# One more transpose per head quad, layer norm sums on VectorE, and another order list, in an interleaved four-layer kernel

## The chip, the cores and the metric

The kernel runs on one core of one Trainium2 chip. The metric is device time in microseconds (us): 3121.67 us is the median of 3 runs before the change (3118.93 to 3122.74). One of these executions, the one of 3118.93 us, was profiled, and all durations below are from that profile.

## The reference

Four layers with residuals act on one sequence of 2048 tokens of 640 numbers, in the order A, B, A, B, with the same weights for both A layers and for both B layers.

```
x = x + _A_ref(_layernorm(x), A_mem0, A_Wq, A_Wk, A_Wv, A_Wo, A_seg_len)
x = x + _B_ref(_layernorm(x), B_wqkv, B_wo)
x = x + _A_ref(_layernorm(x), A_mem0, A_Wq, A_Wk, A_Wv, A_Wo, A_seg_len)
x = x + _B_ref(_layernorm(x), B_wqkv, B_wo)
```

Layer A goes through 64 segments of 32 tokens, one after the other. Each segment has 8 memory rows before it, so 40 rows; q, k and v have 32 heads of 192 numbers; after softmax, weighting and the output projection, the first 8 rows become the memory of the next segment. This chain from segment to segment cannot be cut. Layer B is attention over 8 earlier tokens at distance 0, 2, ..., 14, with 32 heads of 20 numbers.

## The kernel before the change, in words

**Steps.** A loop of 67 steps runs everything (`run`, L841, and `step`, L809). In step t the first A layer works on segment t and, beside it, the second A layer on segment t-2: two lanes of 40 rows, 80 rows in all (`NT`). The B layers of the step before run in the gaps. Steps 0, 1, 64 and 65 have one lane (40 rows); steps 2 to 63 have both; the last step has B alone. Everything is kept transposed: the 640 or 768 features lie on partitions in chunks of 128, the rows run along the free dimension.

**One step of layer A** goes through 8 quads of heads (768 columns of each weight). The pieces, by their names in the list, are: `K`, `Q`, `V` (30 matmuls each, 128x128 weights against 80 rows, L315), their copies out of PSUM `KE` (ScalarE, L341), `QE` (VectorE, L347 and L349) and `VE` (ScalarE, L355 and L357); `T`, transposes of v on TensorE (L369); `TE` and `TF`, which copy the transposed v into its tile `Vt` (VectorE L377 and L379, ScalarE L387); `S`, the scores (6 matmuls, L397); `E`, exp on ScalarE (L403); `EM`, the mask on VectorE (L409); `PO`, probabilities times v (8 matmuls, L430), whose columns of ones in `Vt` give the sums; `R`, one over the sums by Ln and Exp on ScalarE (L417, L419); `OT1` and `OT2`, the scaled outputs on VectorE (L437; L442, L443); `Oa` and `Ob`, the output projection, 15 matmuls each (L449), of which quad 6's second half is cut into `O6x` and `O6y`, and quad 7's into `O7x`, `O7y`, `O7z`. `Oa` of a quad needs rows that `OT1` writes, `Ob` those of `OT2` too. At the end of a step `LSQ`, `lst`, `LMV`, `LR`, `LAP` make the layer norm of the next segment, `MEMa` and `MEMb` (L488) copy the new memory rows into the next step's input, and `X1` adds the residual for layer B. `K0` of the next step can start only when `LAP` and `MEMa` are done. Lower-case pieces are layer B's, from its layer norm (`bsq`, `bst`, `bmv`, `br`, `bap`) over its projections (`bq`, `bk`, `bv`) and attention to `by`.

**Transposes of v before the change.** v of a quad is 6 chunks of 80 rows, 480 columns. Here they are packed into 5 tiles of 128 columns: one chunk (80 columns) is cut into three strips of up to 32, which fill the last 32 columns of three other tiles (the second copy of `vE`). So 5 transposes do. `tF` then moves the three strips to their partitions with three ScalarE copies.

**Layer norm sums before the change.** `ln_sq` (L490) forms the sum of x over the 5 chunks on GpSimd with three additions (L496), and the square and the sum of squares on VectorE (L500, L501); then it splits both sums into high and low halves (L503, L504) for a matmul against ones. In the last step `b_rows` restricts the work to the one lane that is left.

**What sets the order.** Nothing is scheduled by a tool: each engine executes its instructions in the order of the list `ORDER` (L49), one list for all steps with layer A, and `LAST` (L60) for the final step. PSUM tiles rotate through four banks (`big`), and the P·V result and the reciprocal tile have one buffer each.

**Weights.** Layer A's weights are 128 pieces of 256 or 224 KB. 78 stay in SBUF after step 0; the other 50 are read again in every step through a ring of 8 buffers, by DMAs that SyncE issues in the order of use. `resident_pieces` (L97) chooses the 50 so that they lie evenly in the list. So a new list also moves these DMAs.

Of the kernel before, what the change touches and what calls it, by code (L numbers as in the profile page):

```python
# [17 lines left out]
P = 128  # L18
D = 640
# [23 lines left out]
V_AT = (1, 0, 2, 3, 5, 4)  # L43

# [5 lines left out]
K0 bsq K0y KE0 Q0 V0 QE0 bst Q1 S0 bmv VE0 QE1 E0 T0 br K1 TE0 KE1 TF0 V1 Q2 VE1 EM0 S1 PO0 bap QE2 E1 V2 R0  # L50
EM1 T1 K2 VE2 TE1 OT10 bq TF1 OT20 K3 KE2 KE3 bqE PO1 bk R1 K4 S2 KE4 E2 T2 bkE Q3 TE2 bs0 Q4 TF2 bv be0 bvE
OT11 QE3 bs1 be1 EM2 QE4 V3 OT21 eb0 S3 PO2 VE3 E3 eb1 EM3 R2 bt K5 KE5 T3 btE V4 Q5 TE3 TF3 VE4 Oa1 S4 OT12
bp1 OT22 QE5 E4 PO3 on1 EM4 R3 V5 T4 VE5 TE4 K6 OT13 Q6 S5 TF4 OT23 bp0 PO4 KE6 Oa0 Ob0 E5 QE6 on0 T5 R4 S6
TE5 EM5 OT14 E6 V6 TF5 OT24 Q7 QE7 VE6 bo Ob1 PO5 boE T6 by TE6 R5 K7 TF6 byE EM6 KE7 OT15 V7 OT25 VE7 S7 PO6
Oa2 E7 LSQ T7 Ob2 R6 Oa3 EM7 lst TE7 OT16 Ob3 Oa4 TF7 OT26 LMV PO7 Oa6 Oa5 O6x R7 OT17 OT27 Ob4 Ob5 O6y LR LAP
O7x O7y MEMa O7z MEMb X1
# [4 lines left out]
bsq bst bmv br bap bk bkE bq bqE bv bs1 be1 bvE eb1 bt btE bp0 on0 bp1 on1 bo boE by byE  # L61
# [62 lines left out]
class Kernel:  # L124
    def __init__(self, ctx, tc, xT, m0T, wA, wqkv, wo, out):

        self.tc = tc
        self.nc = tc.nc
        self.x = xT
        self.mem0 = m0T  # L130
        self.wA = wA
        self.b_src = (wqkv, wo)
        self.out = out
        self.n_seg = 2 * xT.shape[0]
        pool = lambda name, bufs, **kw: ctx.enter_context(tc.tile_pool(name=name, bufs=bufs, **kw))
        self.cp = pool("consts", 1)
        self.wres = pool("wres", 1)
        self.wring = pool("wring", RING)
        self.ap1 = pool("act1", 1)
        self.ap2 = pool("act2", 2)  # L140
        self.bp = pool("bact", 1)
        self.xp = pool("xio", 1)
        self.ps_one = pool("ps_one", 1, space=PSUM)
        self.units = {}
        self.place = {u: n for n, u in enumerate(half_order())}
        self.resident = resident_pieces()
        self.cur = {}
        self.n_big = 0
        self.bl = range(2)
        self.xt, self.ots, self.qxs, self.kp, self.qp, self.vp, self.tp = {}, {}, {}, {}, {}, {}, {}  # L150
        self.x_load(0)
        self.build_consts()

    def build_consts(self):
# [33 lines left out]
        self.VT = pers("VT", [P, NC, P], 1)[0]  # L188
# [112 lines left out]
    def span_of(self, t):  # L301

        self.l0 = 0 if t < self.n_seg else 1
        self.l1 = 2 if t >= LAG else 1
        self.cs = slice(LT * self.l0, LT * self.l1)
        self.bl = range(2)

    def proj(self, ps, kind, i, h, t, chained=False):

        hT = self.hT[t % 2]  # L310
        c0, c1 = self.cs.start, self.cs.stop
        for k, (c, n) in enumerate(half_blocks(kind, i, h)):
            yield k
            n = V_AT[n] if kind == "v" else n
            self.nc.tensor.matmul(ps[:, NT * n + c0:NT * n + c1], lhsT=self.block(kind, i, h, k), rhs=hT[:, NT * c + c0:NT * c + c1],  # L315
                                  start=(h == 0 and k == 0) if chained else c == 0, stop=(c == NC - 1), skip_group_check=chained)
# [35 lines left out]
    def vE(self, i):  # L352

        ps, cs, copy = self.vp[i], self.cs, self.nc.scalar.copy
        copy(out=self.VT[:, :, cs], in_=ps[:, NT:6 * NT].rearrange("p (a n) -> p a n", a=NC)[:, :, cs])  # L355
        if cs.stop - cs.start == NT:
            copy(out=self.VT[:, 0:3, P - 32:P], in_=ps[:, 0:96].rearrange("p (a n) -> p a n", a=3))  # L357
        else:
            for j in range(3):
                a, b = max(cs.start, 32 * j), min(cs.stop, 32 * (j + 1))  # L360
                if a < b:
                    copy(out=self.VT[:, j, P - 32 + a - 32 * j:P - 32 + b - 32 * j], in_=ps[:, a:b])

    def a_t(self, i):

        nc = self.nc
        ps = self.big("ps_vt", (P, NC, P), BF16)
        for n in range(NC):
            nc.tensor.transpose(out=ps[:, n, :], in_=self.VT[:, n, :], identity=self.ident[:])  # L369
        self.tp[i] = ps  # L370

    def tE(self, i):

        nc = self.nc
        ps = self.tp[i]
        dst = self.Vt[0:NT].rearrange("p (a j e) -> p a j e", a=2, e=P)
        nc.vector.tensor_copy(out=dst[:, :, 0:4:3, :], in_=ps[0:NT, 0:4, :].rearrange("p (a j) e -> p a j e", a=2))  # L377
        two = lambda v: v.rearrange("p (j e) -> p j e", j=2)[:, :, 0:64]
        nc.vector.tensor_copy(out=two(self.Vt[0:NT, 640:896]), in_=ps[0:NT, 4, :].rearrange("p (j e) -> p j e", j=2))  # L379

    def tF(self, i):

        ps = self.tp[i]
        two = lambda v: v.rearrange("p (j e) -> p j e", j=2)[:, :, 0:64]
        for j in range(3):
            n = min(NT - 32 * j, 32)
            self.nc.scalar.copy(out=two(self.Vt[32 * j:32 * j + n, 128:384]), in_=ps[96:96 + n, j, :].rearrange("p (j e) -> p j e", j=2))  # L387
# [102 lines left out]
    def ln_sq(self, x):  # L490

        nc = self.nc
        sq = self.bp.tile([P, NC, NX], BF16, name="sq", tag="sq")
        ns = self.b_rows()
        s = self.bp.tile([P, 4, NX], F32, name="ln_s", tag="xc")
        add = lambda out, a, b: nc.gpsimd.tensor_tensor(out=out, in0=a, in1=b, op=ALU.add)  # L496
        add(s[:, 2:4, ns], x[:, 0:2, ns], x[:, 2:4, ns])
        add(s[:, 2, ns], s[:, 2, ns], s[:, 3, ns])
        add(s[:, 0, ns], s[:, 2, ns], x[:, 4, ns])
        nc.vector.tensor_tensor(out=sq[:, :, ns], in0=x[:, :, ns], in1=x[:, :, ns], op=ALU.mult)  # L500
        nc.vector.tensor_reduce(out=s[:, 1, ns], in_=sq[:, :, ns].rearrange("p c n -> p n c"), op=ALU.add, axis=mybir.AxisListType.X)  # L501
        hl = sq[:].rearrange("p c n -> p (c n)")[:, 0:4 * NX].rearrange("p (j a n) -> p j a n", j=2, a=2)
        nc.vector.tensor_copy(out=hl[:, 0, :, ns], in_=s[:, 0:2, ns])  # L503
        nc.vector.tensor_tensor(out=hl[:, 1, :, ns], in0=s[:, 0:2, ns], in1=hl[:, 0, :, ns], op=ALU.subtract)  # L504
        return hl

    def ln_stats(self, hl):
        nc = self.nc
        ps = self.big("ps_st")
        for j in range(2):  # L510
            nc.tensor.matmul(ps[:, 0:2 * NX].rearrange("p (a n) -> p a n", a=2)[:, :, self.b_rows()], lhsT=self.ones[:], rhs=hl[:, j, :, self.b_rows()],
                             start=(j == 0), stop=(j == 1))
        return ps

    def ln_mv(self, ps):

        nc = self.nc
        ns = self.b_rows()
        m = self.bp.tile([P, NX], F32, name="ln_m")
        nc.vector.tensor_scalar(out=m[:, ns], in0=ps[:, ns], scalar1=1.0 / D, scalar2=None, op0=ALU.mult)  # L520
        v = self.bp.tile([P, NX], F32, name="ln_v")
        nc.vector.tensor_tensor(out=v[:, ns], in0=m[:, ns], in1=m[:, ns], op=ALU.mult)
        nc.vector.scalar_tensor_tensor(out=v[:, ns], in0=ps[:, NX + ns.start:NX + ns.stop], scalar=1.0 / D, in1=v[:, ns], op0=ALU.mult, op1=ALU.subtract)
        return m, v

    def ln_r(self, mv):
# [3 lines left out]
        ns = self.b_rows()  # L530
        nc.scalar.activation(out=v[:, ns], in_=v[:, ns], func=ACT.Ln, bias=self.eps_t[:])
        r = self.bp.tile([P, NX], F32, name="ln_r")
        nc.scalar.activation(out=r[:, ns], in_=v[:, ns], func=ACT.Exp, scale=-0.5)
        return m, r

    def ln_big(self, x, mr, dst):
# [4 lines left out]
        ns = self.b_rows()  # L541
        nc.vector.tensor_tensor(out=xc[:, :, ns], in0=x[:, :, ns], in1=m[:, ns].unsqueeze(1).to_broadcast([P, NC, ns.stop - ns.start]), op=ALU.subtract)  # L542
        for l in self.bl:
# [25 lines left out]
    def b_kE(self, b):  # L569

        o = SEG * (b % 2)
        for l in self.bl:
# [4 lines left out]
    def b_qE(self):  # L577

        self.qx = self.bp.tile([P, NC, BPC, NX], BF16, name="QX", tag="xc")
        ns = self.b_rows()  # L580
        w = ns.stop - ns.start
        q = self.bqp[:, 0:NC * NX].rearrange("p (c n) -> p c n", c=NC)[:, :, ns]
        self.nc.vector.tensor_tensor(out=self.qx[:, :, :, ns], in0=q.unsqueeze(2).to_broadcast([P, NC, BPC, w]),
                                     in1=self.pair_mask[:].unsqueeze(3).to_broadcast([P, NC, BPC, w]), op=ALU.mult)

    def b_rows(self):

        return slice(SEG * self.bl[0], SEG * (self.bl[-1] + 1))
# [198 lines left out]
    def a_piece(self, n, t):  # L787
# [17 lines left out]
        else:  # L805
            {"KE": self.kE, "QE": self.qE, "VE": self.vE, "T": self.a_t, "TE": self.tE, "TF": self.tF, "S": self.a_s, "E": self.sE, "EM": self.sM,
             "R": self.dR, "PO": self.a_pv, "OT1": self.ot1, "OT2": self.ot2}[k](i)

    def step(self, t):  # L809
# [4 lines left out]
        if a:  # L814
            self.span_of(t)
        else:
            self.bl = range(1, 2)
# [85 lines left out]
```

## Time and profile before

| what | value |
|---|---|
| median of 3 runs | 3121.67 us |
| the profiled execution's own time | 3118.93 us |
| its span, first to last instruction | 3117.2 us |
| mean granted TensorE clock | 0.982 |
| matmuls | 82627 |
| VectorE, ScalarE, GpSimd busy | 72%, 71%, 6% |
| DMA engines busy in the steady part | about 87%, 270 GB/s |
| start of step 2, of step 64 | 139.2 us, 3010.0 us |

So the 62 full steps take 2870.8 us, 46.30 us each; the first two steps take 139.2 us, the last three 107.2 us. In a row of the timeline the columns are the start, the duration from the first to the last of the merged instructions, the engine, the line, the operation with its tiles and how many were merged. A matmul's own duration (about 0.2 us) is its way through the array; what it costs in a stream is the distance to the next one's start.

### The profile page before, as it was taken

The numbers are of one execution on the slowest core, as the hardware profiler recorded it, in microseconds if no ns is written. First come the engines' busy times: TensorE is split into PE (matmuls) and PEld (weight loads), VectorE is DVE, ScalarE is ACT, GpSimd is POOL, SyncE is SP. The second block draws the span as 40 slices with busy tenths as digits, with TensorE's granted clock in tenths as the row PEclk, the third lists the DMA queues.
The fourth block names the chain that finished last, engine by engine and source line by source line (L and its number), as shares of the span: only waits on it lengthen the run. The fifth ranks groups of instructions, "written<-read, shape, count | busy, mean of one in ns | idle before, by whom it ended". The sixth has DMA issues, their size and how long they took to land.

```text
span 3117.2 us, 187910 instructions
## 1 busy us (share of the span) xinstructions
PE 3036.5 (97%) x82627; PEld 3009.9 (97%) x82627; DVE 2257.5 (72%) x6748; ACT 2204.5 (71%) x5971; POOL 199.7 (6%) x558
## 2 busy tenths in 40 slices
PE   6899999999999999999999999999999999999997
PEld 5799999999999999999999999999999999999997
DVE  3577777777777777777777777777777777777775
ACT  3477677777777777777777767777777776777764
POOL 3000000000000000000000000000000000000000
PEclk6899999999999999999999999999999999999998
DMA  9988888888888888888888888888888888888886
GB/s 365 319 268 272 270 270 274 273 272 270 271 271 268 271 269 271 273 274 269 271 276 269 272 273 268 269 275 269 270 273 273 270 268 273 267 274 273 270 276 200
DMA packets 497187, 850.95 MB, mean 273 GB/s; under 512 B 55280, under 2 KB 279664, under 8 KB 496368
## 3 DMA queue, kind: packets, MB, share of 16 engines
q1 hardware_dynamic: 487008, 833.67, 84.5%
q8 instruction: 649, 10.63, 1.4%
q10 hardware_dynamic: 9360, 5.26, 0.6%
q14 instruction: 170, 1.39, 0.2%
HBM read 836.09 MB, written 2.62 MB: 269 GB/s over the span
## 4 chain that ended last, share of the span: by engine, by line
PE 87%; DVE 5%; ACT 3%; DMA 3%; issue 1%; SPq 0%; ACTq 0%; POOL 0%; DVEq 0%; POOLq 0%
PE ps_k L315 18%; PE ps_v L315 18%; PE ps_q L315 18%; PE ps_o L430 5%; PE ps_vt L369 5%; PE ps_s L397 5%; ACT R L417 2%; PE ps_bk L565 2%; PE ps_bq L565 2%; PE ps_by L682 2%; PE ps_bv L596 2%; DMA w_ring<-in_wA_dram 1%; PE ps_bs L623 1%; DVE ln_xc L542 1%; DVE OT L437 1%
## 5 line engine op out<-in xcount | busy, mean ns | idle before, releaser
L315 PEld LDWEIGHTS <-w_ring 128*128 128x128 bf16 x18348 | 811.3, 100 | 13.6 <-DMA w_ring<-in_wA_dram 10.6
L417 ACT ACTIVATE R<-ps_o 64x320 f32<-64x320 f32 (+1 forms) x1056 | 449.3, 425 | 122.6 <-PE ps_o L430 91.5
L387 ACT COPY Vt_136<-ps_vt 32x128 bf16<-32x128 bf16 (+1 forms) x1584 | 411.2, 260 | 32.2 <-DVE Vt_136 L379 6.1
L377 DVE COPY Vt_136<-ps_vt 80x512 bf16<-80x512 bf16 x528 | 221.0, 418 | 216.1 <-PE ps_vt L369 215.7
L355 ACT CAST VT_142<-ps_v 128x400 bf16<-128x400 f32 (+1 forms) x528 | 254.7, 482 | 154.5 <-PE ps_v L315 138.7
L403 ACT ACTIVATE Em<-ps_s 80x320 bf16<-80x320 f32 (+1 forms) x528 | 225.8, 428 | 155.6 <-PE ps_s L397 155.5
L437 DVE TENSOR_TENSOR OT<-ps_o,R 128x320 bf16<-128x320 f32 (+1 forms) x528 | 249.8, 473 | 110.5 <-ACT R L419 109.2
L341 ACT CAST KF_123<-ps_k 128x480 bf16<-128x480 f32 (+1 forms) x264 | 144.4, 547 | 253.1 <-PE ps_k L315 217.0
L449 PEld LDWEIGHTS <-w_ring 128*128 128x128 bf16 x6402 | 282.1, 100 | 7.5 <-issue 3.9
L419 ACT ACTIVATE R<-R 128x320 f32<-128x320 f32 (+1 forms) x528 | 244.1, 462 | 16.8
L430 PE MATMUL ps_o<-Em,Vt_136 80*128 80x80 bf16 (+1 forms) x4224 | 237.7, 199 | 3.1 <-issue 3.1
L369 PE MATMUL ps_vt<-ident,VT_142 128*128 128x128 bf16 x2640 | 237.4, 221 | 1.2 <-ACT Em L403 0.9
L347 DVE CAST QT_127<-ps_q 128x320 bf16<-128x320 f32 (+1 forms) x264 | 126.6, 480 | 151.2 <-PE ps_q L315 151.2
L347 DVE CAST QT_129<-ps_q 128x320 bf16<-128x320 f32 (+1 forms) x264 | 127.1, 482 | 115.0 <-PE ps_q L315 107.3
L315 PE MATMUL ps_k<-hT_90,w_ring 128*128 128x80 bf16 (+1 forms) x3531 | 202.3, 201 | 3.1 <-DMA w_ring<-in_wA_dram 2.2
L341 ACT CAST KF_125<-ps_k 128x480 bf16<-128x480 f32 (+1 forms) x264 | 144.4, 547 | 81.5 <-PE ps_k L315 78.3
L315 PE MATMUL ps_q<-hT_90,w_ring 128*128 128x80 bf16 (+1 forms) x3432 | 198.7, 201 | 2.3 <-DMA w_ring<-in_wA_dram 1.6
L315 PE MATMUL ps_k<-hT_92,w_ring 128*128 128x80 bf16 (+1 forms) x3531 | 200.8, 201 | 0.1
L315 PE MATMUL ps_q<-hT_92,w_ring 128*128 128x80 bf16 (+1 forms) x3432 | 197.9, 201 | 2.4 <-DMA w_ring<-in_wA_dram 2.0
L409 DVE TENSOR_TENSOR Em<-Em,maskA 80x320 bf16<-80x320 bf16 (+1 forms) x528 | 163.8, 310 | 29.3 <-ACT Em L403 24.9
L430 PEld LDWEIGHTS <-Vt_136 80*128 80x128 bf16 x4224 | 180.5, 98 | 4.1 <-issue 2.7
L443 DVE TENSOR_TENSOR OT<-ps_o,R 64x160 bf16<-64x160 f32 (+1 forms) x528 | 165.0, 313 | 7.3
(3154 smaller groups left out, 8489.6 us busy)
## 6 DMA issues: line engine op xcount, KB each, us to landing
w_ring<-in_wA_dram SPq DMA_DIRECT2D x1650, 256.0 KB, 4.0
w_ring<-in_wA_dram SPq DMA_DIRECT2D x1650, 224.0 KB, 3.9
out_dram<-YT_94 ACTq DMA_DIRECT2D x32, 80.0 KB, 4.1
wqkv_sb<-in_wqkv_dram SPq DMA_DIRECT2D x3, 800.0 KB, 7.3
wo_sb<-in_wo_dram SPq DMA_DIRECT2D x1, 800.0 KB, 7.6
w_k_00_388<-in_wA_dram SPq DMA_DIRECT2D x1, 256.0 KB, 3.2
w_k_10_407<-in_wA_dram SPq DMA_DIRECT2D x1, 256.0 KB, 3.7
w_q_10_447<-in_wA_dram SPq DMA_DIRECT2D x1, 256.0 KB, 4.3
```

What stands on the lines that cost most here:

```text
L315: self.nc.tensor.matmul(ps[:, NT * n + c0:NT * n + c1], lhsT=self.block(kind, i, h, k), rhs=hT[:, NT * c + c0:NT * c + c1], start=(h == 0 ...
L341: self.nc.scalar.copy(out=kf[:, :, self.cs], in_=self.kp[i][:, 0:6 * NT].rearrange("p (a n) -> p a n", a=6)[:, :, self.cs])
L347: nc.vector.tensor_copy(out=qt[:, :, 0:4:3, cs], in_=pv[:, :, 0:3:2, cs])
L355: copy(out=self.VT[:, :, cs], in_=ps[:, NT:6 * NT].rearrange("p (a n) -> p a n", a=NC)[:, :, cs])
L369: nc.tensor.transpose(out=ps[:, n, :], in_=self.VT[:, n, :], identity=self.ident[:])
L387: self.nc.scalar.copy(out=two(self.Vt[32 * j:32 * j + n, 128:384]), in_=ps[96:96 + n, j, :].rearrange("p (j e) -> p j e", j=2))
L403: self.nc.scalar.activation(out=e[0:NT, :, cs], in_=self.sv[i][0:NT, :, cs], func=ACT.Exp, scale=float(DH) ** -0.5)
L417: self.nc.scalar.activation(out=r[rows, :, :, self.cs], in_=d, func=ACT.Ln)
L419: self.nc.scalar.activation(out=rf, in_=rf, func=ACT.Exp, scale=-1.0)
L430: nc.tensor.matmul(ov[:, pr, b, self.cs], lhsT=vt[0:NT, 512 * pr + P * b:512 * pr + P * (b + 1)], rhs=em[0:NT, 2 * pr + b // 2, self.cs], ...
L437: self.nc.vector.tensor_tensor(out=ot[:, :, 0:3:2, cs], in0=self.ov[:, :, 0:4:3, cs], in1=self.r[i][:, :, :, cs], op=ALU.mult)
L449: self.nc.tensor.matmul(self.acc[c // 3][:, o:o + self.cs.stop - self.cs.start], lhsT=self.block("o", i, h, k), rhs=ot[:, m, self.cs], sta ...
```

## The change

It has four parts.

1. `VT` holds v's 6 chunks as they come. `vE` is one ScalarE copy of 480 columns, `a_t` makes 6 transposes instead of 5, `tE` takes all of them with two VectorE copies (of 512 and 256 columns), and `tF` with its three ScalarE copies is gone.
2. `ln_sq` forms the sum of x on VectorE, with a second reduction like the one over the squares; the three GpSimd additions are gone.
3. `bl` and `b_rows` are gone: the last step works on both lanes, as the others do.
4. `ORDER` and `LAST` are other lists. Among much else, `K1` now follows `K0` directly; `LSQ` stands before `VE7` and `PO6`; and what lies between `PO7` and `O7x` is another set of output chunks.

```diff
 ORDER = """
-K0 bsq K0y KE0 Q0 V0 QE0 bst Q1 S0 bmv VE0 QE1 E0 T0 br K1 TE0 KE1 TF0 V1 Q2 VE1 EM0 S1 PO0 bap QE2 E1 V2 R0
...
-TE5 EM5 OT14 E6 V6 TF5 OT24 Q7 QE7 VE6 bo Ob1 PO5 boE T6 by TE6 R5 K7 TF6 byE EM6 KE7 OT15 V7 OT25 VE7 S7 PO6
-Oa2 E7 LSQ T7 Ob2 R6 Oa3 EM7 lst TE7 OT16 Ob3 Oa4 TF7 OT26 LMV PO7 Oa6 Oa5 O6x R7 OT17 OT27 Ob4 Ob5 O6y LR LAP
-O7x O7y MEMa O7z MEMb X1
+K0 K0y K1 KE0 Q0 bsq V0 KE1 QE0 bst Q1 S0 bmv VE0 QE1 T0 TE0 br V1 E0 EM0 S1 bap Q2 E1 QE2 VE1 EM1 K2 PO0 KE2
...
+EM4 QE6 KE6 V5 T4 OT13 bp0 VE5 OT23 TE4 K5 bp1 PO4 T5 on0 KE5 Ob0 on1 S5 V6 R4 E5 TE5 OT14 OT24 S6 Oa1 E6 bo
+VE6 EM5 boE EM6 Q7 QE7 PO5 T6 R5 by TE6 Ob1 K7 V7 byE KE7 OT15 OT25 LSQ VE7 PO6 R6 Oa2 T7 Ob2 TE7 S7 Oa5 E7
+OT16 OT26 lst Oa6 O6x EM7 PO7 Oa3 LMV Ob3 R7 OT17 Oa4 Ob5 LR O6y OT27 Ob4 O7x LAP MEMa O7y O7z MEMb X1
 """.split()
 LAST = """
-bsq bst bmv br bap bk bkE bq bqE bv bs1 be1 bvE eb1 bt btE bp0 on0 bp1 on1 bo boE by byE
+bsq bst bmv br bap bq bqE bk bkE bs0 be0 bv bs1 be1 eb0 bvE bt eb1 btE bp0 on0 bp1 on1 bo boE by byE
 """.split()
...
-        copy(out=self.VT[:, :, cs], in_=ps[:, NT:6 * NT].rearrange("p (a n) -> p a n", a=NC)[:, :, cs])
-            copy(out=self.VT[:, 0:3, P - 32:P], in_=ps[:, 0:96].rearrange("p (a n) -> p a n", a=3))
...
+        vt = self.VT[:, 0:6 * NT].rearrange("p (a n) -> p a n", a=6)
+        self.nc.scalar.copy(out=vt[:, :, self.cs], in_=self.vp[i][:, 0:6 * NT].rearrange("p (a n) -> p a n", a=6)[:, :, self.cs])
...
-        for n in range(NC):
-            nc.tensor.transpose(out=ps[:, n, :], in_=self.VT[:, n, :], identity=self.ident[:])
+        for n in range(6):
+            nc.tensor.transpose(out=ps[:, n, :], in_=self.VT[:, NT * n:NT * n + P], identity=self.ident[:])
...
+        nc.vector.tensor_copy(out=vt[:, :, 0:4:3, :], in_=src[:, :, 0:3:2, :])
+        nc.vector.tensor_copy(out=vt[:, :, 1:3, 0:64], in_=src[:, :, 1, :].rearrange("p a (j e) -> p a j e", j=2))
...
-    def tF(self, i):
...
-            self.nc.scalar.copy(out=two(self.Vt[32 * j:32 * j + n, 128:384]), in_=ps[96:96 + n, j, :].rearrange("p (j e) -> p j e", j=2))
...
-        add(s[:, 2:4, ns], x[:, 0:2, ns], x[:, 2:4, ns])
-        add(s[:, 2, ns], s[:, 2, ns], s[:, 3, ns])
-        add(s[:, 0, ns], s[:, 2, ns], x[:, 4, ns])
...
+        for j, v in enumerate((x, sq)):
+            nc.vector.tensor_reduce(out=s[:, j, :], in_=v[:].rearrange("p c n -> p n c"), op=ALU.add, axis=mybir.AxisListType.X)
```

## The prediction, on record before the run

> **What bounds the kernel now.** I read the page's first part, then the timeline over one boundary between steps, then the groups by line. The first row says where to look:
>
> ```profile
> PE 3036.5 (97%) x82627; PEld 3009.9 (97%) x82627; DVE 2257.5 (72%) x6748; ACT 2204.5 (71%) x5971; POOL 199.7 (6%) x558
> ```
>
> TensorE is busy 97% of the span, VectorE and ScalarE under three quarters. A share does not say whether matmuls lie back to back, so the timeline has to (step 9 begins with the first row, step 10 with the last):
>
> ```profile
> 464.35 0.45 PE L315 MATMUL ps_k<-hT_92,w_k_00_388 128*128 128x80 bf16 x8
> ...
> 474.19 0.45 PE L369 MATMUL ps_vt<-ident,VT_142 128*128 128x128 bf16 x5
> 474.47 0.45 PE L315 MATMUL ps_k<-hT_92,w_ring 128*128 128x80 bf16 x8
> ...
> 506.10 0.46 PE L430 MATMUL ps_o<-Em,Vt_136 80*128 80x80 bf16 x8
> ...
> 506.65 0.88 ACT L417 ACTIVATE R<-ps_o 64x320 f32<-64x320 f32 x2 [0.85 <-PE ps_o L430]
> ...
> 508.06 0.49 DVE L437 TENSOR_TENSOR OT<-ps_o,R 128x320 bf16<-128x320 f32 x1 [1.24 <-ACT R L419]
> ...
> 508.79 0.32 DVE L443 TENSOR_TENSOR OT<-ps_o,R 64x160 bf16<-64x160 f32 x1
> ...
> 509.08 0.45 PE L449 MATMUL ps_acc_16129<-OT,w_ring 128*128 128x80 bf16 x8
> 509.14 0.49 DVE L542 TENSOR_TENSOR ln_xc<-xin_86,ln_m 128x320 f32<-128x320 bf16 x1
> 509.37 0.42 PE L449 MATMUL ps_acc_16129<-OT,w_o_01_1979 128*128 128x80 bf16 x7
> ...
> 509.91 0.42 PE L449 MATMUL ps_acc_16130<-OT,w_o_11_1998 128*128 128x80 bf16 x7
> 510.21 0.20 DVE L488 CAST hT_90<-ps_acc_16129 128x48 bf16<-128x48 f32 x1
> 510.36 0.19 DVE L488 CAST hT_90<-ps_acc_16130 128x32 bf16<-128x32 f32 x1
> 510.46 0.45 PE L315 MATMUL ps_k<-hT_90,w_k_00_388 128*128 128x80 bf16 x8
> ```
>
> Three readings. The step takes 510.46-464.35 = 46.11 us. A weight chunk costs (509.37-509.08)/8 = 36 ns, a transpose (474.47-474.19)/5 = 56 ns. And the last 7 chunks are issued by 509.91+0.25 = 510.16, so TensorE stands 0.30 us at the boundary, for a chain that begins when PO7 is issued (506.39): R7, OT17, OT27, layer norm, the new memory rows, K0. Elsewhere in this step TensorE's rows follow each other without a gap. So the step is bound by TensorE's own work plus one wait of 0.30 us. The 62 full steps average 46.30, 0.19 above this one: some steps hold pauses of 0.1 to 1 us, which the waits put down mostly to "issue".
>
> **The change, part by part.**
>
> *One more transpose.* 8 in a step at 56 ns: +0.45 us in each full step, 62 x 0.45 = 27.8 us, with nothing beside it, since TensorE has no gap. (The Trainium skill, page "TensorE: Matmul & The Clock Gate", section "Back-to-back issue gap", speaks harder against the change: about 81 ns for each 128-column matmul with its weight load in a real stream. It would make 40 us of the 496 transposes. The row above shows 56 ns in just such a stream, so the row decides.)
>
> *The copies around the transposes.* These rows go or change:
>
> ```profile
> L387 ACT COPY Vt_136<-ps_vt 32x128 bf16<-32x128 bf16 (+1 forms) x1584 | 411.2, 260 | 32.2 <-DVE Vt_136 L379 6.1
> L357 ACT CAST VT_142<-ps_v 128x96 bf16<-128x96 f32 x496 | 121.3, 245 | 0.0
> L379 DVE COPY Vt_136<-ps_vt 80x128 bf16<-80x128 bf16 x528 | 110.8, 210 | 0.0
> L501 DVE TENSOR_REDUCE ln_s<-sq 128x64 f32<-128x320 bf16 x131 | 93.1, 711 | 4.5
> ```
>
> ScalarE loses three copies of 260 ns and, per quad, 492+245 becomes one copy like K's (480 columns, 559 ns): about 0.96 us a quad, 7.7 of its 33.5 us a step. VectorE's second copy grows from 128 to 256 columns, to about 280 ns between its 210 and the 418 of 512 columns: +0.6 us a step. I count ScalarE's relief at nothing: no wait of TensorE in an ordinary step ends on it but R7's, which starts 0.26 us after PO7 already and does not move.
>
> *Layer norm sums.* Two more reductions of 0.71 us a step, so VectorE has 34.2+0.6+1.4 = 36.2 us in 46.5. Its 0.6 us waits for GpSimd (66 of them, 40.5 us) go, to no one's gain: at the first layer norm the list now puts 120 chunks (4.3 us) ahead of `bst`, and sums ending 3.1 us after K0's start hide there. (The skill's page "VectorE: DVE Perf Modes", section "Rules for kernel authors", calls the reduction VectorE's slowest operation, to be avoided on a hot path. The trace agrees: 711 ns against 325 for the square of the same 320 columns. What that is worth depends on where it queues.)
>
> *Where it queues.* In the new list `LSQ` stands on VectorE ahead of TE7, OT16, OT26 and EM7, and Oa6 waits for OT16, PO7 for EM7. Let P be the end of PO6's issue. ScalarE starts VE7 at P-0.09 (0.20 after V7's last chunk, as at 502.60 in the trace), and can start R6 some 0.45 to 0.59 later, at P+0.36 to P+0.50; OT16 may follow 1.41 after that (506.65 to 508.06): P+1.77 to P+1.91. VectorE ends OT25 at P-1.1 (2.72 after PO5's issue as in 506.39 to 509.11, 0.2 later for `byE` before it, and 4.04 of matmuls from PO5 to PO6); the sums take 0.36+0.71+0.81+0.26+0.29 = 2.43, to P+1.3; TE7's two copies 0.65, so OT16 starts at P+1.95 and ends at P+2.44. TensorE comes to Oa6 after Oa2, T7, Ob2, S7, Oa5 and lst, 0.54+0.34+0.54+0.28+0.54+0.11 = P+2.35. A new wait of 0.13 us; PO7 then finds EM7 done to within 0.03. I take +0.12 a step, between 0 (VectorE's instructions overlap more) and 0.4 (each of the five sums 50 ns later).
>
> *The boundary.* Between PO7 and O7x now stand Oa3, Ob3, Oa4, Ob5, O6y, Ob4: 81 chunks instead of 75, and with O7 111 instead of 105. The chain is the same (LMV moves behind PO7, but its 0.75 us end before OT17 at 1.67), so the 0.30 us shrink by 6 x 36 ns: -0.22 a step, between 0 and -0.30. Of the wait that remains, MEMa and LAP are last, as now.
>
> *DMAs.* As many pieces are streamed (50); the list re-chooses which. In full steps no wait for a weight DMA is listed from 300 to 3000 us, so I count 0; if pieces bunch, up to +0.3 a step. The first two steps run at 365 GB/s, DMA-bound with the same bytes: 0, at most +1 us.
>
> *One-lane steps and the last one.* Steps 64 and 65 take at most 2 x 0.45 more; partly they wait for weights: +0.5. In the last step everything is a chain, and there both lanes cost. Sums: 2.43 instead of the 1.56 from 3097.97 to 3099.53: +0.9. Small layer norm operations in full width and a second multiplication in `bap`: +0.5. bqE in full width (1.48) and two bkE halves then end about as late as bv's matmuls did: 0. But `bs0 be0` come before `bs1 be1`, which now wait for bv (1.33 at the halved clock), and `bvE` behind both exps:
>
> ```profile
> 3106.21 1.19 ACT L629 ACTIVATE EB_144<-ps_bs 64x512 bf16<-64x512 f32 x2 [5.14 <-PE ps_bs L623]
> 3107.42 0.43 ACT L603 CAST VTB_380<-ps_bv 128x320 bf16<-128x320 f32 x1
> ```
>
> From the scores' start at 3105.45 that is 2.4 us to the end of bvE now; then 0.28+1.33+0.76+1.19+0.43 = 4.0: +1.6. Together +3.0, between 2 and 4.
>
> **Sum.** A full step: 0.45-0.22+0.12 = +0.35, 62 x 0.35 = 21.7; +0.5; +3.0: 25.2 us. On the profiled execution's 3118.93 that is 3144.1. The median is 2.7 above that execution, and a new median may lie as much above its best: I take 3145.
>
> **Rivals.**
>
> *No new wait, and the boundary closes:* +0.15 to +0.23 a step, 9 to 14, and 3 for the ends: 3132 (3126 to 3136). For it: ScalarE is freer, and OT16's wait is only 0.13 by sums of many rows. Against: Oa6 really has nothing to spare. 0.17.
>
> *VectorE's queue or the weights bind:* wait of 0.4 at Oa6, or pieces that land late in the dense start of the step (K0, K1, Q0, V0, Q1): +0.28 more a step, 17 us: 3163 (3156 to 3175). For it: VectorE gets all of the new work, in one lump before the tightest place. 0.19.
>
> *Faster:* the pauses put down to "issue" go. They make 62 x 0.19 = 11.8 us in the full steps and some 5 in step 64 (2.1, 1.4, 1.3 and 0.6); ScalarE has 2,144 instructions fewer, and if fetching instructions is what stops TensorE, this falls. With the whole boundary wait gone too and no new one, a full step changes by 0.45-0.30-0.19 = -0.04, and with -5 for step 64 and +3.5 for the ends the kernel comes out at 3115. It decides only where nearly all pauses go: each 0.1 that stays in a step is worth 6.2 us. Against: the pauses stand in TensorE's own queue, and its instructions grow. 0.04.
>
> The forecast itself (3137 to 3155) has 0.60. A run of this kernel tells 0.2%, 6.2 us, from no change. Within that lies the lower end of the first rival, 0.05; faster 0.04; slower 0.91. The range for 8 in 10 leaves out the faster end and the upper half of the second rival: 3131 to 3164.
>
> **What would show it.** Step length from K0 to K0 in the timeline: 46.46 in a quiet step. Six transposes in 0.34 us. A gap of about 0.08 before K0 and one of about 0.1 at the first output chunks of quad 6, whose releaser is the VectorE product after R. ScalarE near 26 us a step, GpSimd only its input copies. From the last K0 to the end 3 us more. I am wrong if quiet steps differ from 46.46 by over 0.15, or if the span changes while they do not.

## The result, and the profile after

The changed kernel takes 3151.83 us, the median of 3 runs (3151.60 to 3152.07), against 3121.67: a ratio of 1.0098 with a 95% interval of 1.0076 to 1.0121. The prediction was 3145 with a range of 3131 to 3164, so the run lies 6.8 above the forecast and inside the range. The profiled execution has a span of 3149.9 us, 32.7 above the 3117.2 of before.

The first row of the page after:

```profile
PE 3071.2 (98%) x83160; PEld 3042.6 (97%) x83160; DVE 2385.2 (76%) x6883; ACT 1747.4 (55%) x3829; POOL 48.5 (2%) x162
```

ScalarE has fallen from 71% to 55%, VectorE has risen from 72% to 76%, GpSimd does its input copies only, and TensorE is as full as it was. Now the timeline of one quiet step, from its K0 (first row) to the next (last row):

```profile
610.83 0.45 PE L309 MATMUL ps_k<-hT_90,w_k_00_386 128*128 128x80 bf16 x8
...
648.48 0.33 DVE L471 TENSOR_TENSOR sq<-xin_88 128x320 bf16<-128x320 bf16 x1
...
649.28 0.46 PE L407 MATMUL ps_o<-Em,Vt_134 80*128 80x80 bf16 x8
...
649.34 0.70 DVE L474 TENSOR_REDUCE ln_s<-sq 128x64 f32<-128x320 bf16 x1
649.48 0.56 ACT L348 CAST VT_140<-ps_v 128x480 bf16<-128x480 f32 x1 [0.52 <-PE ps_v L309]
...
649.57 0.27 PE L426 MATMUL ps_acc_20493<-OT,w_o_00_1688 128*128 128x80 bf16 x3
...
650.06 0.88 ACT L394 ACTIVATE R<-ps_o 64x320 f32<-64x320 f32 x2
...
650.33 0.29 DVE L477 TENSOR_TENSOR sq<-ln_s,sq 128x128 bf16<-128x128 f32 x1
...
650.98 0.47 ACT L396 ACTIVATE R<-R 128x320 f32<-128x320 f32 x1
...
650.99 0.28 DVE L364 COPY Vt_134<-ps_vt 80x256 bf16<-80x256 bf16 x1
...
651.48 0.49 DVE L414 TENSOR_TENSOR OT<-ps_o,R 128x320 bf16<-128x320 f32 x1 [0.22 <-ACT R L396]
...
651.80 0.28 PE L484 MATMUL ps_st<-sq,ones 128*128 128x128 bf16 x2
...
652.02 0.27 PE L426 MATMUL ps_acc_20493<-OT,w_o_00_1770 128*128 128x80 bf16 x3
...
656.95 0.42 PE L426 MATMUL ps_acc_20494<-OT,w_o_11_1963 128*128 128x80 bf16 x7
657.04 0.20 DVE L465 CAST hT_92<-ps_acc_20493 128x48 bf16<-128x48 f32 x1
657.29 0.38 PE L309 MATMUL ps_k<-hT_92,w_k_00_386 128*128 128x80 bf16 x6
```

The step is 657.29-610.83 = 46.46 us. At the boundary, the last 7 chunks are issued by 656.95+0.25 = 657.20 and K0 starts at 657.29: 0.09 us instead of 0.30. The two matmuls of `lst` start at 651.80 and take 0.11 in the stream, but quad 6's first output chunk starts only at 652.02: the new gap of 0.11. OT16 (L414) ends just before it, and its own idle time names R on ScalarE (L396), not VectorE's queue; that row decides a point below. R6 itself (650.06) has no idle time before it: it starts when VE7 (649.48 + 0.56 = 650.04) leaves ScalarE.

To compare whole runs I cut each trace at its K0 starts. "Quiet" is the tenth percentile of the 62 full steps; "pauses" is what all 62 have above that, summed. us throughout:

| trace | start of step 2 | 62 full steps | quiet step | pauses | step 64 | step 65 and last | span |
|---|---|---|---|---|---|---|---|
| before | 139.2 | 2870.8 | 46.11 | 11.8 | 42.9 | 64.3 | 3117.2 |
| after | 142.1 | 2897.3 | 46.46 | 16.9 | 44.5 | 66.0 | 3149.9 |
| before, second trace | 136.8 | 2885.4 | 46.11 | 26.4 | 44.1 | 64.5 | 3130.8 |
| after, second trace | 136.5 | 2898.2 | 46.45 | 18.0 | 45.1 | 67.8 | 3147.6 |

Of the 32.7 us between the first two traces, 62 x 0.345 = 21.4 are quiet steps, 5 are pauses, 2.9 the start, 3.2 the end. The second pair shows what of this belongs to the change: the quiet steps come again to 0.01 us. The pauses do not: 11.8 and 26.4 in one and the same kernel before. The start does not either. (The second traces are from chips 2 and 11; the chip of the first pair is not on record.)

A quiet step by what TensorE works on (from the first instruction on a tile to the next on another, so a gap counts with the tile before it; mean of some 40 steps before and 30 after):

| tile | before | after | difference |
|---|---|---|---|
| transposes of v, `ps_vt` | 2.253 | 2.708 | +0.455 |
| `ps_st`, with the gap before Oa6 | 0.228 | 0.339 | +0.111 |
| output chunks `ps_acc`, with the gap before K0 | 8.955 | 8.733 | -0.222 |
| all others | 34.68 | 34.68 | 0.00 |

That is all of the +0.344, and the three terms are the three of the prediction. One figure did not move: from PO7's start to the next K0 both kernels take 4.36 us (mean of the quiet steps).

### The profile page after: what moved, and what is told of

Read it like the earlier page. It is cut to its first block, busy times and chain, and to the rows that moved or that the text cites. A ratio compares the mean times of both kernels' runs of the same rounds, so it can differ in the third digit from the quotient of the medians.

```text
span 3149.9 us, 186002 instructions
## 1 busy us (share of the span) xinstructions
PE 3071.2 (98%) x83160; PEld 3042.6 (97%) x83160; DVE 2385.2 (76%) x6883; ACT 1747.4 (55%) x3829; POOL 48.5 (2%) x162
## 3 DMA queue, kind: packets, MB, share of 16 engines
q8 instruction: 651, 10.67, 1.4%
## 4 chain that ended last, share of the span: by engine, by line
PE 95%; DMA 3%; issue 1%; DVE 1%; ACT 0%; SPq 0%; DVEq 0%; ACTq 0%
PE ps_k L309 18%; PE ps_q L309 18%; PE ps_v L309 18%; PE ps_vt L355 6%; PE ps_o L407 5%; PE ps_s L374 5%; PE ps_bq L534 2%; PE ps_by L645 2%; PE ps_bk L534 2%; PE ps_bv L559 2%; PE ps_bs L586 1%; DMA w_ring<-in_wA_dram 1%; PE ps_bo L609 1%; PE ps_bvt L572 1%; PE ps_st L484 0%
## 5 line engine op out<-in xcount | busy, mean ns | idle before, releaser
L348 ACT CAST VT_140<-ps_v 128x480 bf16<-128x480 f32 (+1 forms) x528 | 287.0, 544 | 308.6 <-PE ps_v L309 242.8
L414 DVE TENSOR_TENSOR OT<-ps_o,R 128x320 bf16<-128x320 f32 (+1 forms) x528 | 251.9, 477 | 134.4 <-ACT R L396 117.9
L355 PE MATMUL ps_vt<-ident,VT_140 128*128 128x128 bf16 x3168 | 268.7, 221 | 3.2 <-issue 2.7
L396 ACT ACTIVATE R<-R 128x320 f32<-128x320 f32 (+1 forms) x528 | 244.0, 462 | 16.8
L355 PEld LDWEIGHTS <-VT_140 128*128 128x128 bf16 x3168 | 191.2, 99 | 3.8 <-issue 3.8
L309 PE MATMUL ps_v<-hT_90,w_ring 128*128 128x80 bf16 (+1 forms) x3003 | 172.5, 201 | 4.5 <-DMA w_ring<-in_wA_dram 3.5
L309 PE MATMUL ps_q<-hT_92,w_ring 128*128 128x80 bf16 (+1 forms) x3003 | 172.1, 201 | 4.9 <-DMA w_ring<-in_wA_dram 4.1
L309 PE MATMUL ps_q<-hT_90,w_ring 128*128 128x80 bf16 (+1 forms) x3003 | 172.8, 201 | 2.6 <-DMA w_ring<-in_wA_dram 2.1
L309 PE MATMUL ps_v<-hT_92,w_ring 128*128 128x80 bf16 (+1 forms) x3003 | 171.9, 201 | 2.5 <-issue 2.4
L309 PE MATMUL ps_k<-hT_90,w_ring 128*128 128x80 bf16 (+1 forms) x2970 | 171.1, 201 | 2.1 <-DMA w_ring<-in_wA_dram 1.6
```

What stands on the lines that cost most here:

```text
L348: self.nc.scalar.copy(out=vt[:, :, self.cs], in_=self.vp[i][:, 0:6 * NT].rearrange("p (a n) -> p a n", a=6)[:, :, self.cs])
L355: nc.tensor.transpose(out=ps[:, n, :], in_=self.VT[:, NT * n:NT * n + P], identity=self.ident[:])
L396: self.nc.scalar.activation(out=rf, in_=rf, func=ACT.Exp, scale=-1.0)
L414: self.nc.vector.tensor_tensor(out=ot[:, :, 0:3:2, cs], in0=self.ov[:, :, 0:4:3, cs], in1=self.r[i][:, :, :, cs], op=ALU.mult)
```

## The experiments

All ratios are to runs of the kernel before on the same chip. Its own median was 3114.1 us on chip 0 (the first four experiments), 3129.0 on chip 11 (the boundary, the hybrid, no streaming, the second trace of after) and 3129.3 on chip 2 (the others), so times of different chips are compared only with this in mind.

### Six transposes alone

```diff
 (kernel before, its list without TF0 to TF7)
-        for n in range(NC):
-            nc.tensor.transpose(out=ps[:, n, :], in_=self.VT[:, n, :], identity=self.ident[:])
+        for n in range(6):
+            nc.tensor.transpose(out=ps[:, n, :], in_=self.VT[:, NT * n:NT * n + P], identity=self.ident[:])
```

> The kernel before, with its own list and its sums on GpSimd, only with six transposes per quad, one ScalarE copy for V and no copies by ScalarE behind the transposes. By the theory (a transpose costs 56 ns with nothing beside it, and ScalarE's relief is worth nothing): quiet step 46.11 + 0.45 = 46.56 us, the gap before K0 still 0.30, GpSimd as before, ScalarE near 26 us a step; 62 x 0.45 = 28 us and about 0.5 at the end: 3150 us. By a first rival (relief of ScalarE lets R7 or OT27 come earlier and the boundary wait shrinks): quiet step 46.3 to 46.45, 3135 to 3143. By a second (81 ns a transpose, as the Trainium skill has it, page "TensorE: Matmul & The Clock Gate", section "Back-to-back issue gap"): quiet step above 46.7, 3162.

Measured: 3135.31 us, ratio 1.0062 (1.0042 to 1.0081). Quiet step 46.50 (+0.39), pauses 5.4, gap before K0 unchanged. Averaged over the quiet steps, and counted from the first transpose of a quad to the next instruction, the transposes take 2.700 us a step instead of 2.253: 8 for 0.447, 56 ns each, as the theory has it. (The 81 ns of the Trainium skill's "Back-to-back issue gap", page "TensorE: Matmul & The Clock Gate", are not seen; the trace decides.) The missing 0.06 is a small wait that went: before PO7, TensorE stood 0.05 us for OT26 in the kernel before, and no longer; R6, at the head of that chain, now starts 0.55 us behind the end of PO6's issue instead of 0.62. So ScalarE's relief was worth 0.05 us a step there, and nothing at the boundary. The first rival is refuted at its place. The total is below the 3150 expected because it holds fewer pauses, and the kernel before ran at 3114 on this chip.

### The sums on the old list

```diff
 (kernel after, ORDER and LAST of before without TF0 to TF7)
```

> The kernel after with the list of before (its copies by ScalarE left out): six transposes and layer norm sums on VectorE in full width, but the output chunks of quad 6 behind PO7 and the layer norm sums at their old place. By the theory the quiet step is 46.56 plus a new wait at PO7: VectorE has OT25, the sums (2.43), EM7, TE7, OT16, OT26 in a row, OT26 would end near 3.4 us after PO6 and TensorE comes to PO7 after 3.15: 0.25 to 0.35, so 46.8 to 46.9 us, gap before K0 0.30; 62 x 0.74 = 46 us and 3 for the ends: 3170 us. By the rival (VectorE's instructions overlap, the sums are hidden on any list): 46.56, 3153.

Measured: 3140.10 us, ratio 1.0079 (1.0056 to 1.0102). Quiet step 46.55, 0.05 above the run before; that is all at PO7, for OT26. I expected 0.25 to 0.35, so my count of VectorE's queue was too long by over 0.2, and the rival (sums nearly hidden on any list) is closer.

### The sums back on GpSimd, new list

```diff
+        add(s4[:, 2:4], x[:, 0:2], x[:, 2:4])
+        add(s4[:, 2], s4[:, 2], s4[:, 3])
+        add(s4[:, 0], s4[:, 2], x[:, 4])
-        for j, v in enumerate((x, sq)):
-            nc.vector.tensor_reduce(out=s[:, j, :], in_=v[:].rearrange("p c n -> p n c"), op=ALU.add, axis=mybir.AxisListType.X)
+        nc.vector.tensor_reduce(out=s4[:, 1], in_=sq[:].rearrange("p c n -> p n c"), op=ALU.add, axis=mybir.AxisListType.X)
```

> The kernel after with the sums of x back on GpSimd (full width), list and six transposes as in after. By the theory (Oa6 waits 0.13 for OT16 because the sums stand ahead of it on VectorE): VectorE has 0.7 less ahead of OT16, which then follows R6 and ends 2.26 to 2.40 after PO6, against 2.35 for Oa6: the wait falls to 0 to 0.05, quiet step 46.33 to 46.38, 62 x 0.1 = 6 us less than after: 3145. By the rival (R6 on ScalarE ends last whatever VectorE does): wait 0.12 as before, quiet step 46.46, 3151. A third: GpSimd beside VectorE makes VectorE's instructions longer and the step is above 46.46.

Measured: 3145.68 us, ratio 1.0094 (1.0072 to 1.0116); quiet step 46.45, the same as after. Its timeline at quad 6's first output chunks:

```profile
503.84 0.56 ACT L348 CAST VT<-ps_v 128x480 bf16<-128x480 f32 x1 [0.52 <-PE ps_v L309]
...
504.43 0.88 ACT L394 ACTIVATE R<-ps_o 64x320 f32<-64x320 f32 x2
...
505.33 0.47 ACT L396 ACTIVATE R<-R 128x320 f32<-128x320 f32 x1
...
505.35 0.28 DVE L364 COPY Vt<-ps_vt 80x256 bf16<-80x256 bf16 x1
...
505.84 0.49 DVE L414 TENSOR_TENSOR OT<-ps_o,R 128x320 bf16<-128x320 f32 x1 [0.21 <-ACT R L396]
...
506.16 0.28 PE L488 MATMUL ps_st<-sq,ones 128*128 128x128 bf16 x2
...
506.38 0.48 PE L426 MATMUL ps_acc<-OT,w_o 128*128 128x80 bf16 x9
```

The gap (506.16+0.11 to 506.38) is there as in after, with 0.7 us less work ahead of OT16. VectorE has been idle 0.21 us and waits for R. My theory of this wait falls: the sums do not make it. The rival holds: R6 on ScalarE ends last whatever VectorE does. What holds R6 is not PO6 but ScalarE's own queue: VE7, the copy of V7, ends at 504.40 and R6 starts at 504.43, 0.50 us behind the end of PO6's issue (503.93), with no idle time before it. VE7, the three operations of R6 and OT16 in a row take longer than the chunks that the list puts between PO6 and `Oa6`. No run moves VE7 behind R6, so whether that alone would close the gap is not shown.

### Five transposes on the new list

```diff
 (kernel after, with vE, a_t, tE, tF and V_AT of before)
+ORDER: TF0 behind E0, TF1..TF3 behind R0..R2, TF4 behind VE5, TF5 behind KE5, TF6 behind R5, TF7 behind E7
```

> The kernel after with the five transposes and ScalarE's copies of before, on the new list; the copies stand behind E0, R0, R1, R2, VE5, KE5, R5 and E7. By the step of the prediction that counts ScalarE's relief at nothing: quiet step 46.46 - 0.45 = 46.01 us, 3123. By the rival (in the new list the copies, about 1 us each, stand ahead of something that TensorE waits for: PO's Vt, R and so the next PO or the output chunks): new waits at PO and Oa6 of together 1 to 2 us, quiet step 47 to 48, 3190 to 3250. I hold the rival the likelier, since PO_i needs all of Vt and this list leaves less between T_i and PO_i.

Measured: 3275.16 us, ratio 1.051 (1.0489 to 1.0531), quiet step 48.70, beyond the 47 to 48 that I expected of the rival. Its waits of TensorE from 300 to 3000 us:

```profile
PE ps_o L422 <- DVE OT L435: 35.8, 55, 0.9
PE ps_o L422 <- DVE Vt L369: 31.1, 56, 0.6
PE ps_acc L441 <- DVE OT L429: 15.9, 55, 0.3
PE ps_v L307 <- ACT Vt L379: 11.3, 52, 0.2
```

Each row gives the total, the number of waits and the longest, in us. The fourth row is ScalarE's copies into `Vt` (L379), which the new kernel no longer has. The second is VectorE's first copy (L369), which the new kernel has too; it is late because the places of ScalarE's copies are mine, and one is poor: TF4 stands ahead of TE4, and TE4 then waits 1.8 us for it. The first and third are outputs that come late; what held them is not followed here. So the run shows that this list cannot simply take the copies back, and not what they would cost at their best.

### The boundary alone

```diff
-OT16 Ob3 Oa4 TF7 OT26 LMV PO7 Oa6
+OT16 Ob3 O4x TF7 OT26 LMV PO7 O4y Oa6
+            for c in (range(9) if n[2] == "x" else range(9, 15)):
+                self.o_mm(4, 0, c)
```

> The kernel before, with only the last 6 chunks of Oa4 moved from ahead of PO7 to behind it, so that 81 instead of 75 chunks stand between PO7 and O7's first. By the theory: gap before K0 0.30 - 0.22 = 0.08; TensorE comes to PO7 0.22 earlier, where OT26 has been done for only about 0.1, so a new wait of 0.05 to 0.15 there: quiet step 45.95 to 46.05 us, 3112 to 3118. By the rival (what sets K0 is not the chain from PO7: LAP or the pieces of K0): gap stays 0.30, quiet step 46.11, 3122.

Measured: 3135.88 us, ratio 1.0014 (1.0003 to 1.0025); quiet step 46.11, as before. The timeline shows the end of PO6's issue (first row), PO7 and the boundary of one step:

```profile
508.23 0.46 PE L453 MATMUL ps_acc<-OT,w_ring 128*128 128x80 bf16 x8
...
508.38 0.44 ACT L407 ACTIVATE Em<-ps_s 80x320 bf16<-80x320 f32 x1
...
508.84 0.88 ACT L421 ACTIVATE R<-ps_o 64x320 f32<-64x320 f32 x2
...
510.98 0.32 DVE L447 TENSOR_TENSOR OT<-ps_o,R 64x160 bf16<-64x160 f32 x1
511.05 0.20 PE L453 MATMUL ps_acc<-OT,w_o 128*128 128x80 bf16 x1
...
511.36 0.46 PE L434 MATMUL ps_o<-Em,Vt 80*128 80x80 bf16 x8
...
511.65 0.67 PE L453 MATMUL ps_acc<-OT,w_o 128*128 128x80 bf16 x14
...
511.90 0.88 ACT L421 ACTIVATE R<-ps_o 64x320 f32<-64x320 f32 x2 [0.85 <-PE ps_o L434]
...
515.38 0.42 PE L453 MATMUL ps_acc<-OT,w_o 128*128 128x80 bf16 x7
515.47 0.20 DVE L492 CAST hT<-ps_acc 128x48 bf16<-128x48 f32 x1
515.72 0.38 PE L319 MATMUL ps_k<-hT,w_k 128*128 128x80 bf16 x6
```

Before K0 0.09 us are left of 0.30, as the theory has it. But TensorE comes to PO7 at 511.09, and OT26 ends at 511.30: the wait there is 0.27 us now instead of 0.05. All of the 0.22 has gone from one gap to the other. In the means of the quiet steps, PO6 to PO7 takes 3.42 us and PO7 to K0 4.36, in this kernel as in the kernel before. So what binds is a chain of latencies over R6, OT16 and OT26 to PO7, and on over R7, OT17 and the last chunks to K0; where the filling chunks stand only chooses the gap that shows it. Its first link is ScalarE's queue: R7, which finds ScalarE idle, starts 0.25 us behind the end of PO7's issue (511.65 to 511.90), but R6 starts 0.61 behind PO6's (508.23 to 508.84), when E7 (508.38 + 0.44) is out of its way. I expected PO7 to take 0.05 to 0.15 of it; the step came out where the rival had it, but not for the rival's reason, since the gap before K0 did close.

### A hybrid: six transposes in quad 7 alone

```diff
 (the run before, without TF7, lst behind Ob3)
+        m, w = (6, NT) if i == 7 else (NC, P)
+        for n in range(m):
+            nc.tensor.transpose(out=ps[:, n, :], in_=self.VT[:, w * n:w * n + P], identity=self.ident[:])
```

> The kernel before with the 6 chunks moved as in the run before, and quad 7 alone with six transposes, one copy for V and no copies by ScalarE behind them; quads 0 to 6 keep five. By the theory: +0.056 for one transpose, -0.22 at the boundary, and ScalarE, 0.18 us sooner at R6, brings OT26 in time for PO7: quiet step 46.11 - 0.22 + 0.06 = 45.95 us, 62 x -0.16 = -10: 3111 us, faster than both. By the rival (another wait takes the place: lst or bst for the sums, PO7 for OT26): 46.05 to 46.15, 3117 to 3124.

Measured: 3130.08 us against 3129.02, ratio 0.9999 (0.9989 to 1.0010). Quiet step 46.04, 0.07 shorter; the wait at PO7 is 0.14, before K0 0.09. That is where the rival had it, not at the 45.95 of the theory. The chain from PO6 to PO7 got 0.07 shorter (3.35 instead of 3.42), as R6 starts 0.07 sooner (0.55 behind PO6 instead of 0.62); the wait at PO7 fell by 0.13, because the sixth transpose (0.056) now fills part of it. Pauses are 27.6 us, and the gain of 4.5 us does not show. A run below takes them away.

### No streaming, and half of it

```diff
         if u in self.units:
             v = self.units[u]
+        elif self.t > 1:
+            v = next(self.units[x] for x in self.units if x[3] == q)
 (half of it: the condition is self.t > 1 and (u[1] + h) % 2)
```

> The kernel after, which from step 2 on loads no weights any more: every piece that would be streamed is read from a resident tile of the same size, so the matmuls, their number and order are the same with other weights (the output is not the reference's). TensorE's pauses put down to "issue" make 16.8 us in the 62 full steps of after. By the theory that they come from the weights' transfers getting in the way of TensorE's instruction fetch: they go, nearly all steps 46.46, 62 full steps 2880.5 instead of 2897.3, 3134 us. By the rival (the pauses belong to TensorE's own instruction stream): the steps keep a mean near 46.73 and the time stays at 3150. A quiet step under 46.46 would say that transfers cost quiet steps too.

> The kernel after, which from step 2 on streams 25 of its 50 pieces a step; the others are read from resident tiles (the output is not the reference's). DMA engines then stand near 45% instead of 86%. By the theory that an instruction fetch is late where it comes behind a queue of weights: pauses fall to a tenth or two of after's 17 us, under 3.5, since with half of the load a fetch seldom meets a queue. By the rival (each transfer that meets a fetch costs the same): half of them, 8 to 9 us. Quiet step 46.46 in both.

Measured, without streaming: 3116.90 us, ratio 0.9957 (0.9944 to 0.9970). With half of it (one run): 3125.33 us. For the first I expected 3134. One row each for 300 to 3000 us, with TensorE's busy time, its granted clock, the DMA engines' share and GB/s. After:

```profile
300.00:3000.00 2700.00, 2691.68 (x72827) 1.00 0.86 270
```

After, half of the pieces streamed:

```profile
300.00:3000.00 2700.00, 2700.00 (x73229) 1.00 0.50 138
```

After, none streamed:

```profile
300.00:3000.00 2700.00, 2700.00 (x73231) 1.00 0.02 5
```

The pauses are 16.9, 1.0 and 0.7 us, with the same matmuls at the same clock. The chips bear it out: 18.0 in the second trace of after against 0.7 on chip 11, and 26.4 in the second trace of before against 1.0 with half of the streaming on chip 2. So they come with the weights' streaming, and not in proportion: at half of the traffic they are nearly gone. Quiet steps are 46.46, 46.46 and 46.45, so traffic costs a quiet step nothing. The spans of after with and without streaming differ by 34.5; what is not pauses, and what my 3134 left out, is at the end: step 64 takes 35.6 instead of 44.5, step 65 and the last 56.9 instead of 66.0.

### Both kernels, and the hybrid, without streaming

The same edit on the kernel before and on the hybrid, and second traces of before and after.

> The kernel before, which from step 2 on reads every streamed piece from a resident tile of the same size, as the run on after did (the output is not the reference's). Without pauses the two kernels differ by the change alone. By the theory of the step sum: all 62 full steps 46.11, 2859 us, against 2880.8 in after; the steps of one lane and the last one 2 to 4 us shorter than after's 35.6 + 56.9: a span near 3115.4 - 22 - 3 = 3090 us. By the rival (part of the 32 us between the two kernels was the way that their transfers fall): the same 22 in the full steps, but under 1 us at the end, 3093; or the full steps differ by less than 18.

> The hybrid (six transposes in quad 7 alone, 6 chunks of Oa4 behind PO7), without streaming from step 2 on (the output is not the reference's). Its quiet step was 46.04, 0.07 under before's, but 27.6 us of pauses hid that. By the theory: all full steps 46.04, 62 x 0.07 = 4.5 us under the kernel before without streaming, about 3085. By the rival (the 0.07 exists in quiet steps only by choice of the steps): no difference of over 2 us.

> The kernel after once more, for its second trace: quiet step 46.46; does the first stage (142.1 us to the third K0, against 139.2 before) come out the same, and the pauses (16.8 us against 11.7)? If they scatter by several us from run to run they say nothing of the change; if they come again at the same places they belong to it.

> The kernel before once more, for its second trace beside these: quiet step 46.11; first two steps 139 or, as they scattered by 5.6 us between the two traces of after, 136 to 142; pauses 11.8 if they belong to the program, up to 25 if chip and run decide.

| without streaming | start of step 2 | 62 full steps | quiet step | step 64 | step 65 and last | span |
|---|---|---|---|---|---|---|
| before | 138.8 | 2860.4 | 46.12 | 36.7 | 53.6 | 3089.6 |
| after | 142.0 | 2880.8 | 46.45 | 35.6 | 56.9 | 3115.4 |
| hybrid | 138.4 | 2855.8 | 46.05 | 36.4 | 54.8 | 3085.4 |

Medians: before 3092.88 (ratio 0.9885, 0.9865 to 0.9905), hybrid 3086.68 (0.9864, 0.9849 to 0.9879). The spans of 3090 and 3085 that I expected of the theory came out. Almost without pauses (about 1 us in each) the change costs 25.8 us of span: 20.4 in the full steps, 3.3 in the last two, 3.2 at the start, -1.1 in step 64. (After was on chip 11 and before on chip 2; the medians differ by 24.0.) The hybrid's 4.6 us in the full steps show in this pair of traces; the medians' intervals overlap.

The second traces (one run each, 3149.36 after and 3132.55 before) are in the first table. The row of the kernel before, second trace, beside after's above:

```profile
300.00:3000.00 2700.00, 2678.77 (x72691) 1.00 0.87 270
```

The kernel before stood idle longer here than after did. Pauses scatter from run to run (or from chip to chip) by more than the 5 us between the first two traces, so those 5 us cannot be put down to the change.

## Why the prediction was right, and where not

- **The time.** 3145 was forecast, from a sum of +25.2. Without streaming the spans differ by +25.8, of which 3.2 are the start; the runs shown have +30.2 between medians, with 5 us of pauses and 3 us of start that come and go. That 3145 stood 2 below its own sum (3144.1 plus the 2.7 of the median) is a rounding by judgement that the run did not bear out.
- **The transposes: right.** +0.45 a step forecast, 2.708-2.253 = +0.455 measured, and +0.447 alone.
- **The boundary: right in size.** -0.22 forecast, -0.222 measured, of which 0.21 before K0. But the reason given (6 more chunks) holds only together with the rest: alone they give nothing. The way from PO7 to K0 is 4.36 us in every kernel where it was measured, so chunks behind PO7 help only if PO7 is also reached without a new wait; in after it waits 0.05 for its predecessors, as in before.
- **The wait at Oa6: right size, wrong cause.** +0.12 forecast, +0.111 measured. The step that failed: VectorE's sums keep OT16 until 1.95 us behind PO6. The term that was too long is their 2.43 us, which took 2.14 (648.48 to 650.33+0.29). VectorE is free at 651.27 (650.99+0.28), 1.70 behind the end of PO6's issue (649.57); R6 ends at 651.45 and OT16 starts at 651.48, 1.91 behind. The prediction had this other path, VE7 and then R6 on ScalarE, at 1.77 to 1.91 behind PO6, just below the path it chose; it is the one that binds, by the run with GpSimd's sums. TensorE's arrival at Oa6 was right: 2.34 (651.80+0.11) against 2.35. The two paths were 0.04 to 0.18 apart, within what a sum of ten rows can tell.
- **ScalarE's relief at nothing: nearly right.** 0.05 us a step on the old list, at PO7. But the reason given, that no wait but R7's hangs on ScalarE, was not: two of the waits, at PO7 in before and at Oa6 in after, hang on R6, which stands in ScalarE's queue behind E7 or VE7 (0.62 us behind PO6 in before, 0.50 in after, where R7 stands 0.25 behind PO7). What the relief is worth on the new list stays open.
- **VectorE's sums hidden at the first layer norm: right** for full steps (no gap there in a quiet step). At the second one they cost 0.05 on the old list, at PO7.
- **DMAs 0 in full steps: right** for quiet steps. **"Issue" pauses unchanged: not wrong, but not a constant.** They are 11.8 or 26.4 us in the same kernel. The rival that let them vanish with ScalarE's instructions is refuted: after has 2,142 fewer and no fewer pauses. Its guess that fetching instructions is what stops TensorE fits the traces (last section); the instructions are TensorE's own.
- **First two steps: 0 to 1 forecast.** 136.8 to 139.2 in three traces of before (one of them without streaming), 136.5 to 142.1 in four of after (two with less streaming, which starts at step 2): 2 us more on average. Why is open.
- **The ends: +0.5 for steps 64 and 65 and +3.0 for the last one forecast, 3.5 together.** Measured for step 64, and for step 65 with the last: -1.1 and +3.3 without streaming, +1.5 and +1.7 in the first pair. The last step can be followed. Kernel before without streaming, then after without streaming:

```profile
3071.18 0.24 DVE L502 TENSOR_TENSOR sq<-x 128x160 bf16<-128x160 bf16 x1
...
3074.69 1.00 PE L567 MATMUL ps_bk<-h2T,wqkv_sb 128*128 128x64 bf16 x25 [1.71 <-DVE h2T L546]
...
3080.13 0.43 ACT L605 CAST VTB<-ps_bv 128x320 bf16<-128x320 f32 x1
...
3086.78 0.34 ACTq L708 DMA_DIRECT2D out_dram<-YT  x1
```

```profile
3094.59 0.33 DVE L473 TENSOR_TENSOR sq<-x 128x320 bf16<-128x320 bf16 x1
...
3099.06 1.49 PE L536 MATMUL ps_bq<-h2T,wqkv_sb 128*128 128x64 bf16 x25 [2.10 <-DVE h2T L515]
...
3106.23 0.43 ACT L568 CAST VTB<-ps_bv 128x320 bf16<-128x320 f32 x1
...
3112.88 0.34 ACTq L671 DMA_DIRECT2D out_dram<-YT  x1
```

From the square to the output: 15.60 and 18.29, +2.7 (forecast +3.0). Up to the projections +0.96 (forecast 0.9+0.5), from there to bvE +1.73 (forecast +1.6), then the same 6.65 in both.

So the likeliest case came true, by its own terms. One of its causes was another, and the total agrees this well partly by chance: the pauses alone differ by 15 us between two traces of the kernel before.

## What to carry to other kernels

Where the bounding engine is full, an instruction more on it costs its full issue distance: here 0.45 us a step, of which the relief of the other engines gave back 0.06. A gap on it that ends a chain of latencies cannot be filled by moving filler work past one link of the chain: shorten the chain (as the hybrid does), or look for the gap at the link before. Look for the first link in the queues of the engines that are not full: work that is needed later can stand ahead of what the chain needs now, as VE7 does ahead of R6 here (moving it was not tried). When two paths end within 0.2 us of each other, name both and test which binds; and before a few microseconds are given to a change, look at a second trace of the same kernel, on the same chip.

## What the runs showed of the hardware

TensorE's pauses put down to "issue" depend on the DMA load: 1.0 us in 62 steps at a DMA share of 0.50, 3.4 to 27.6 us in the kernels with full streaming, at 0.83 to 0.87. The page of after shows what they wait for:

```profile
q1 hardware_dynamic: 487008, 837.93, 84.1%
q8 instruction: 651, 10.67, 1.4%
```

Queue q8 carries 10.67 MB of instructions in 651 packets of 16,384 bytes, one every 4.8 us, and 10.67 MB over the 2 x 83160 matmuls and weight loads is 64 bytes for each. In before it is 10.63 MB over 2 x 82627, 64 bytes again. So I take it for TensorE's own stream.

The traces hold the time of every packet, and that ties the pauses to them. The 62 full steps of all fourteen traces have 267 pauses put down to "issue" with more than 0.2 us from one matmul's start to the next. Each of them ends 1.20 to 1.63 us after a packet of q8 has ended; of moments taken at random 9% do. So in these pauses TensorE starts again when its instructions have come, and the runs with less streaming show that they come late only beside the weights' transfers. How a packet gets late is not shown: those before a pause took 0.92 to 0.97 us themselves (medians), as the others do in the kernels with full streaming.

What decides between 3.4 us of pauses (the sums on the old list) and 27.6 (the hybrid), at nearly the same share, stays open. The chip is a rival that no run separates from the kernel: the four traces of chip 0 have 3.4 to 10.2 us, the three of chip 11 with full streaming 18.0 to 27.6, the one of chip 2 has 26.4. (The Trainium skill, page "CRC Debugging", section "Comparing the Two Runs", names queue 14 for the refill of instructions; this trace has 149 packets there, and the 651 on queue 8.)
